# Attention and conv FFN on one core: z as [hi;hi] and [lo;lo], diagonal triangle transposed, planes landing as words

## The chip, the cores and the metric

One core of one Trainium2 chip runs the whole problem. The metric is device time in microseconds. The kernel before takes 1581.85 us, the median of three runs from 1581.26 to 1582.96.

## The reference, cut to what matters

For each of 4 batches, with S = 3136 positions, 256 value columns and 64 columns in z:

```python
scores = (1/S) * z @ z.T
attn   = maximum(scores, 0) ** 2
x      = u * (attn @ v)
h      = maximum(x @ w_in, 0)                  # 256 -> 1024
c      = conv of h along S, three taps per column (conv_w)
out    = (h * sigmoid(c)) @ w_out              # 1024 -> 256
```

The scores are symmetric: the score of key i for query j is that of key j for query i.

## The kernel before

A batch is cut into 6 blocks of 512 queries and a remainder of 64. The 24 blocks follow each other. Each meets 25 tiles of 128 keys (the last holds 64 keys twice), one tile a slot: 600 slots in all. Every fp32 operand of a matmul is split into a high part that TensorE takes in one pass and a low part (x - high); products are hi*hi, hi*lo and lo*hi, the scores all four.

z lies feature by partition. `za` holds [hi;lo] over its 128 partitions and `zb` holds [lo;hi], so that two matmuls, `za` and `zb` as weights against `za` as moving operand, sum all four products (`scores`, L290 and L291). `prep_z` (L158) fills them by half tiles of 64 partitions.

A tile is computed or transposed. A computed one has `scores`, `relu` (L342, ScalarE, PSUM bank s to SBUF tile t), `square` (L353, VectorE, or ScalarE in some early slots), `split_hi` (L360, ScalarE, tile ah), `split_lo` (L366, by the helper at L143, VectorE, tile al) and `attend` (L382, six matmuls into the two av banks). A tile whose mirror image an earlier block has already computed is taken from there. When that earlier block had its relu tile, `part` (L310, GpSimd) cut its fp32 words into two planes of 16-bit halves, pl, and `spill` (L320) wrote them to a DRAM tile dq, one plane behind the other. Later `fetch` (L328) brings the tile back by a transposing DMA of 16-bit elements into tp, with the two planes side by side, and `join` (L334, GpSimd) weaves the halves into words, tj. From these ScalarE makes the square in a PSUM bank (L339) and ah (L358); no scores matmul is needed. The tiles on the diagonal, four of each block, are computed in full.

`entries` (L110) gives the order of tiles in a block: the half tile first, the transposed ones spread evenly among the computed ones. In block q of a batch 4q tiles are transposed (fewer in the first batch, whose blocks 1 to 3 compute the first four key tiles again).

Each slot of the loop at L865 issues, in this order: `split_hi` and `split_lo` of slot k+2, `relu` and `square` of k+3, the planned work of the slot, `fetch` of k+9, `join` of k+5, `part` of k+2, `spill` of k+1, then `attend` of k and `scores` of k+4. Each engine works through its own share in that order, and so does the queue of SyncE, which issues nearly all DMAs. The framework adds the waits. A tile with a tag takes one of that tag's `bufs` buffers, and its first writer waits until one is free: s has 2, ah and al 4, t, pl, tp and tj 3 each.

The FFN of block b runs inside block b+1: `gate_x` (L490) and `split_x` (L512) turn av into xh and xl, the two xl halves on GpSimd; then eight groups of columns pass `ffn_in` (L531 to L534), relu, three taps, sigmoid, gate, split and `ffn_out` (L604 to L606). The 64 remaining queries of a batch are gathered by `rem_fetch`, `rem_join`, `rem_scores` and others around the last block. `tail` plans the end.

Of the kernel before, what the change touches and what calls it, by code (L numbers as in the profile page):

```python
# [8 lines left out]
F32 = mybir.dt.float32  # L9
# [19 lines left out]
LA, LT, LS = 4, 3, 2  # L29
LD, LJ, LP, LX = 9, 5, 2, 1  # L30

# [28 lines left out]
T_XL = "VV"  # L60

R_F, R_J, R_D, R_U, R_T = -14, -10, -12, -6, 13


@with_exitstack
def kernel(
# [43 lines left out]
    def entries(b, q):  # L110
        n, m = q * CB, min(own(b, q), q * CB)
        cs, ts = list(range(m)) + list(range(n, NJ)), list(range(m, n))
        if b or q:
            cs.insert(0, cs.pop())
        n = len(ts)
        return [
            (ts.pop(0), True) if (i + 1) * n // NJ > i * n // NJ else (cs.pop(0), False)
            for i in range(NJ)
        ]

# [5 lines left out]

    za = const.tile([P, NJ * P], F32R, name="za")
    zb = const.tile([P, NJ * P], F32R, name="zb")
    vv = const.tile([P, NJ, 2, D], F32R, name="vv")
# [27 lines left out]

    def prep_z(q, half):  # L158
        c = slice(q * NB, min((q + 1) * NB, S))
        t = zst.pop(q) if half else zst[q]  # L160
        g = nc.gpsimd
        if half == 0:
            copy(nc.scalar, za[LO, c], t[LO])
            sub(g, zb[LO, c], t[LO], za[LO, c])
            return
        copy(nc.scalar if q % 2 else nc.vector, zb[HI, c], t[HI])
        sub(g, za[HI, c], t[HI], zb[HI, c])
        if q == QB:

            for x in (za, zb):  # L170
                g.tensor_copy(x[:, S : S + HALF], x[:, S - HALF : S].bitcast(F32))

    def first_z():
        t, h = zst.pop(0), P
        v, g = nc.vector, nc.gpsimd
        c = slice(0, NB)
        copy(nc.scalar, zb[HI, c], t[HI])
        copy(v, za[LO, c], t[LO])
        sub(v, za[HI, c], t[HI], zb[HI, c])
        sub(g, zb[LO, :h], t[LO, :h], za[LO, :h])  # L180
        sub(v, zb[LO, h:NB], t[LO, h:], za[LO, h:NB])

# [111 lines left out]
    rl, pl, dq, tp, tj = {}, {}, {}, {}, {}  # L294


    def rows_of(b, r):
        if (b, r) not in dq:
            n, c = (NB, r * NB) if r < QB else (RQ, RB * NB)
            dq[b, r] = dr.tile([2, n, c], U16, tag=f"dq{r}", name=f"dq{r}")  # L300
        return dq[b, r]

    def part(k):
        blk, j, tr = at_slot(k)
        b, q = divmod(blk, QB)
        r = j // CB
        if tr or r < (Q0 if b == q == 0 else q + 1) or (r == QB and q >= RB):
            return
        pl[k] = wk.tile([P, 2, NB], U16, tag="pl", name="pl", bufs=3)
        nc.gpsimd.tensor_copy(pl[k], rl.pop(k).bitcast(U16).rearrange("p (n h) -> p h n", h=2))  # L310

    def spill(k):
        blk, j, _ = at_slot(k)
        b, q = divmod(blk, QB)
        if k not in pl:
            return
        r, p = j // CB, pl.pop(k)
        a, n = j * P - r * NB, min(P, S - j * P)
        d = rows_of(b, r)[:, a : a + n, q * NB : (q + 1) * NB]
        nc.sync.dma_start(out=d.rearrange("h p n -> p h n"), in_=p[:n])  # L320

    def fetch(k):
        blk, j, tr = at_slot(k)
        b, q = divmod(blk, QB)
        if tr:
            tp[k] = wk.tile([P, 1, 2 * NB], U16, tag="tp", name="tp", bufs=3)
            src = rows_of(b, q)[:, :, j * P : (j + 1) * P].rearrange("h r c -> (h r) c")
            nc.sync.dma_start_transpose(tp[k], src)  # L328

    def join(k):  # L330
        if k in tp:
            t = tp.pop(k)[:, 0].rearrange("p (h n) -> p h n", h=2)
            tj[k] = wk.tile([P, NB], F32, tag="tj", name="tj", bufs=3)
            nc.gpsimd.tensor_copy(tj[k].bitcast(U16).rearrange("p (n h) -> p h n", h=2), t)  # L334
# [50 lines left out]

    rt, rs, rr = {}, {}, {}
    RN = [range(i * CB, min(i + 2, RB) * CB) for i in range(0, RB, 2)] + [range(RB * CB, NJ)]

    def rem_picks():
        t = wk.tile([P, RQ], F32, tag="tj", name="pk", bufs=3)  # L390
        nc.gpsimd.memset(t, 0.0)
# [11 lines left out]
    def rem_fetch(b, i):  # L403
        n = len(RN[i])
        rt[i] = wk.tile([P, n, 2 * RQ], U16, tag="pl", name="rt", bufs=3)
        c = RN[i][0] * P
        nc.sync.dma_start_transpose(rt[i], rows_of(b, QB)[:, :, c : c + n * P].rearrange("h r c -> (h r) c"))

    def rem_join(i):
        n = len(RN[i])  # L410
        rs[i] = t = wk.tile([P, NB], F32, tag="t", name="rj", bufs=3)[:, : n * RQ]
        nc.gpsimd.tensor_copy(
            t.bitcast(U16).rearrange("p (c n h) -> p c h n", h=2, n=RQ),
            rt.pop(i).rearrange("p c (h n) -> p c h n", h=2),
        )

    def rem_scores(i):
        p = ps.tile([P, 512], F32, tag="ph", name="ph", bufs=2)
        r = za[:, QB * NB : S]
        for x, j in enumerate(RN[i]):  # L420
            w, o = slice(j * P, (j + 1) * P), p[:, x * RQ : (x + 1) * RQ]
            nc.tensor.matmul(o, lhsT=za[:, w], rhs=r, start=True, stop=False)
            nc.tensor.matmul(o, lhsT=zb[:, w], rhs=r, start=False, stop=True)
        rr["p"] = p
# [115 lines left out]
    def ffn_halo(blk, f):  # L540
        if blk == "r":
            hb[blk, f] = t = wk.tile([P, RW], F32, tag="tj", name="hr", bufs=3)
            nc.gpsimd.tensor_copy(seam(t)[:, :, 0:2], ends[:, f])
# [109 lines left out]
    for q in range(2, QB + 1):  # L653
        s = 4 * q - LA - 3 if q < QB else 4 * QB - LA - 4
        at(max(s - 4, -LA), POST, load_z, 0, q)
        at(s, POST, prep_z, q, 0)
        at(s, POST, prep_z, q, 1)
    at(-3, POST, prep_z, 1, 0)
    at(-3, POST, prep_z, 1, 1)
    for j in range(2, NJ, 2):  # L660
# [191 lines left out]
    with tc.manual_schedule():  # L852
# [12 lines left out]
        for k in range(-LA, NS):  # L865
# [79 lines left out]
```

## Time and profile before

| | |
|---|---|
| median of three runs | 1581.85 us |
| time of the profiled execution | 1582.39 us |
| its span, first to last instruction | 1580.5 us |
| its instructions | 22342 |
| chain that ended last: TensorE, ScalarE, GpSimd, VectorE | 83%, 7%, 4%, 3% |
| DMA packets, bytes | 352826, 175.70 MB |

The profiled execution lies 1.9 us over its span and 0.5 us over the median. A busy share counts the time in which an engine has an instruction in work; instructions of TensorE overlap, so that the mean duration of one is longer than the distance from one to the next.

### The profile page before, as it was taken

Reading aid. Unit: us, or ns where it says so; the run is one execution under the profiler, and the core shown is the slowest. Engines: PE = TensorE matmul, PEld = TensorE weight load, DVE = VectorE, ACT = ScalarE, POOL = GpSimd, SP = SyncE. Lnnn points to the kernel's source line nnn. Section 1 sums busy time; section 2 is a strip of 40 time slices with the busy share of each in tenths; the row PEclk is TensorE's granted clock in tenths of the full one; section 3 lists DMA queues with packets and bytes.
Section 4 is the critical chain, followed back from the end, with each engine's and each line's share of the span. In section 5 each row is a group of like instructions: output and inputs, shape, how many; then the busy total and the mean of one; then the engine's idle time right before and its main releaser. Section 6 shows DMA issues by size and latency. Waiting matters only on the chain.

```text
span 1580.5 us, 22342 instructions
## 1 busy us (share of the span) xinstructions
PE 1558.8 (99%) x6868; PEld 1275.0 (81%) x6868; DVE 1093.0 (69%) x1680; ACT 1244.3 (79%) x2329; POOL 1109.1 (70%) x1325
## 2 busy tenths in 40 slices
PE   8999999999999999999999999999999999999998
PEld 6677887878888888888888888887888888888787
DVE  7787776656777766656777776665677777666567
ACT  8898777878777877878877777787887777778767
POOL 7675567977866766778775676777875666767753
PEclk9999999999999999999999999999999999999999
DMA  5432434554434445456343444454633334546521
GB/s 162 130 120 64 117 81 112 136 124 105 140 102 122 114 87 132 106 126 138 97 141 97 110 119 105 126 113 94 155 109 111 114 93 125 105 93 133 103 54 35
DMA packets 352826, 175.70 MB, mean 111 GB/s; under 512 B 260545, under 2 KB 337345, under 8 KB 352705
## 3 DMA queue, kind: packets, MB, share of 16 engines
q1 hardware_dynamic: 352032, 173.88, 43.8%
q8 instruction: 53, 0.87, 0.2%
q14 instruction: 69, 0.56, 0.1%
q10 hardware_dynamic: 672, 0.40, 0.1%
HBM read 36.59 MB, written 75.24 MB: 71 GB/s over the span
## 4 chain that ended last, share of the span: by engine, by line
PE 83%; ACT 7%; POOL 4%; DVE 3%; issue 2%; DMA 0%; POOLq 0%; ACTq 0%; DVEq 0%
PE av L382 42%; PE ph L534 5%; PE o L606 5%; PE o L604 5%; PE s L290 5%; PE o L605 5%; PE ph L531 5%; PE ph L532 5%; PE s L291 5%; PE av L447 1%; POOL xl L143 1%; POOL tj L334 1%; DVE ph L573 1%; ACT t L342 1%; DVE al L143 1%
## 5 line engine op out<-in xcount | busy, mean ns | idle before, releaser
L382 PE MATMUL av<-ah,vv 128*128 128x512 f32 x2400 | 739.6, 391 | 4.6 <-DVE ut L499 1.9
L143 DVE TENSOR_TENSOR al<-s,ah 128x512 fp32r<-128x512 f32 x576 | 397.7, 690 | 272.3 <-ACT ah L358 203.9
L382 PEld LDWEIGHTS av<-ah,vv 128*128 128x128 f32 x2400 | 449.3, 188 | 102.5 <-DVE ut L499 2.7
L382 PE MATMUL av<-al,vv 128*128 128x512 f32 x1152 | 449.7, 390 | 0.8 <-DVE al L143 0.6
L353 DVE TENSOR_TENSOR s<-s,t 128x512 f32<-128x512 f32 x350 | 244.2, 698 | 175.4 <-ACT t L342 174.0
L334 POOL COPY tj<-tp 128x1024 uint16<-128x1024 uint16 x228 | 307.8, 1359 | 0.0
L342 ACT ACTIVATE t<-s 128x512 f32<-128x512 f32 x372 | 222.6, 598 | 101.3 <-PE s L291 88.5
L360 ACT CAST ah<-s 128x512 fp32r<-128x512 f32 x372 | 218.9, 588 | 102.1 <-DVE s L353 101.4
L573 DVE SCALAR_TENSOR_TENSOR ph<-hb,cw,ph 128x512 f32<-128x512 f32 x384 | 287.0, 747 | 7.4 <-ACT ph L568 6.7
L143 POOL TENSOR_TENSOR gl<-hb,gh 128x512 fp32r<-128x512 f32 x192 | 248.7, 1295 | 52.6 <-ACT gh L146 51.1
L310 POOL COPY pl<-t 128x1024 uint16<-128x1024 uint16 x248 | 256.5, 1039 | 7.6 <-DMA dq<-pl 7.1
L382 PEld LDWEIGHTS av<-al,vv 128*128 128x128 f32 x1152 | 216.5, 188 | 48.8 <-DVE al L143 3.9
L563 POOL COPY halo<-hb 128x2 f32<-128x2 f32 x160 | 30.1, 188 | 208.1 <-ACT hb L558 207.2
L290 PE MATMUL s<-za 128*128 128x512 f32 x372 | 148.7, 400 | 9.7 <-DVE za L143 5.1
L531 PE MATMUL ph<-xh,wih 128*128 128x512 f32 x384 | 149.8, 390 | 0.6 <-DVE hb L587 0.6
L532 PE MATMUL ph<-xh,wil 128*128 128x512 f32 x384 | 149.6, 390 | 0.0
L604 PE MATMUL o<-gh,wol 128*128 128x512 f32 x384 | 149.6, 390 | 0.0
L605 PE MATMUL o<-gh,woh 128*128 128x512 f32 x384 | 149.5, 389 | 0.0
L606 PE MATMUL o<-gl,woh 128*128 128x512 f32 x384 | 149.5, 389 | 0.0
L339 ACT ACTIVATE s<-tj 128x512 f32<-128x512 f32 x228 | 136.5, 599 | 15.7 <-POOL tj L334 15.7
L291 PE MATMUL s<-za,zb 128*128 128x512 f32 x372 | 145.9, 392 | 0.0
L358 ACT ACTIVATE ah<-tj 128x512 fp32r<-128x512 f32 x228 | 143.4, 629 | 0.3
(113 smaller groups left out, 2031.1 us busy)
## 6 DMA issues: line engine op xcount, KB each, us to landing
dq<-pl SPq DMA_DIRECT2D x228, 256.0 KB, 2.5
vst<-in_v_dram SPq DMA_DIRECT2D x48, 256.0 KB, 3.1
ut<-in_u_dram SPq DMA_DIRECT2D x24, 512.0 KB, 4.3
out_dram<-ob SPq DMA_DIRECT2D x19, 512.0 KB, 3.6
st<-in_z_dram SPq DMA_DIRECT2D x24, 256.0 KB, 3.1
tp<-dq SPq DMA_TRANSPOSE x228, 3.4
dq<-pl SPq DMA_DIRECT2D x20, 128.0 KB, 2.6
wr<-in_moe_w_in_dram SPq DMA_DIRECT2D x8, 256.0 KB, 3.1
```

The source lines that it names most:

```text
L143: eng.tensor_tensor(out=out, in0=a, in1=b.bitcast(F32), op=ALU.subtract)
L310: nc.gpsimd.tensor_copy(pl[k], rl.pop(k).bitcast(U16).rearrange("p (n h) -> p h n", h=2))
L334: nc.gpsimd.tensor_copy(tj[k].bitcast(U16).rearrange("p (n h) -> p h n", h=2), t)
L342: nc.scalar.activation(rl[k], sc[k][:, :NB], AF.Relu, scale=SC1)
L353: nc.vector.tensor_tensor(out=s, in0=s, in1=rl[k], op=ALU.mult)
L382: nc.tensor.matmul(o, lhsT=w[:, j, d], rhs=r, start=first and i == 0, stop=last and i == len(ops) - 1)
L531: nc.tensor.matmul(o, lhsT=wih[:, dc, w], rhs=xh[blk][:, dc], start=(dc == 0), stop=False)
L532: nc.tensor.matmul(o, lhsT=wil[:, dc, w], rhs=xh[blk][:, dc], start=False, stop=False)
L573: nc.vector.scalar_tensor_tensor(out=c, in0=hb[blk, f][:, k : e + k], scalar=cw[:, f, k : k + 1], in1=c, op0=ALU.mult, op1=ALU.add,)
L604: nc.tensor.matmul(o, lhsT=wol[:, f, d], rhs=h, start=(f == 0), stop=False)
L605: nc.tensor.matmul(o, lhsT=woh[:, f, d], rhs=h, start=False, stop=False)
L606: nc.tensor.matmul(o, lhsT=woh[:, f, d], rhs=l, start=False, stop=(f == FC - 1))
```

## The change

z is kept as `zh` = [hi;hi] and `zl` = [lo;lo]: `prep_z` needs one copy on ScalarE and one subtraction on GpSimd over 128 partitions in place of two of each kind over 64. The moving operand [hi;lo] of a block becomes a tile of its own, `zq`, which two DMAs from `zh` and `zl` fill eight slots before the block. In every block but the first, the four diagonal tiles stand at slots 1, 8, 15 and 22 of the block. Diagonal tile x computes only the columns from 128x on; the columns left of the diagonal are those of the earlier diagonal tiles, spilled to a DRAM tile `below` and fetched by a transposing DMA (`fetch_side`, five slots ahead). The DRAM tiles keep the two halves of a row next to each other, so that the transposed halves land as words; `join` and `rem_join` go. `fetch` runs eight slots ahead, tp has five buffers. The x tile of the gate joins the ring t, and one xl half goes from GpSimd to VectorE.

```diff
-LD, LJ, LP, LX = 9, 5, 2, 1
+LD, LE, LP, LX, LB = 8, 5, 2, 1, 5
+DG = [1, 8, 15, 22]
+ZQ = 4
...
     def entries(b, q):
         n, m = q * CB, min(own(b, q), q * CB)
-        cs, ts = list(range(m)) + list(range(n, NJ)), list(range(m, n))
-        if b or q:
-            cs.insert(0, cs.pop())
...
+        if not b and not q:
+            return [(j, False) for j in range(NJ)]
+        fixed = {0: NJ - 1, **{p: n + x for x, p in enumerate(DG)}}
+        cs, ts = list(range(m)) + list(range(n + CB, NJ - 1)), list(range(m, n))
...
+    def side(k):
+        blk, j, tr = at_slot(k)
+        x = j - blk % QB * CB
+        return x if blk and not tr and 0 <= x < CB else None
...
-    def prep_z(q, half):
+    def prep_z(q):
         c = slice(q * NB, min((q + 1) * NB, S))
...
+        t, g = zst.pop(q), nc.gpsimd
+        copy(nc.scalar, zh[:, c], t)
+        sub(g, zl[:, c], t, zh[:, c])
...
+    def query(blk):
+        b, q = divmod(blk, QB)
+        zq[blk] = t = mv.tile([P, NB], F32R, tag="zq", name="zq", bufs=2)
+        c = slice(q * NB, (q + 1) * NB)
+        nc.sync.dma_start(out=t[LO].bitcast(F32), in_=zh[LO, c].bitcast(F32))
+        nc.sync.dma_start(out=t[HI].bitcast(F32), in_=zl[HI, c].bitcast(F32))
...
-        w = slice(j * P, (j + 1) * P)
-        r = za[:, blk % QB * NB : (blk % QB + 1) * NB]
-        nc.tensor.matmul(s, lhsT=za[:, w], rhs=r, start=True, stop=False)
-        nc.tensor.matmul(s, lhsT=zb[:, w], rhs=r, start=False, stop=True)
+        w, c = slice(j * P, (j + 1) * P), (side(k) or 0) * P
+        r = zq[blk][:, c:]
+        nc.tensor.matmul(s[:, c:], lhsT=zh[:, w], rhs=r, start=True, stop=False)
+        nc.tensor.matmul(s[:, c:], lhsT=zl[:, w], rhs=r, start=False, stop=True)
...
-            dq[b, r] = dr.tile([2, n, c], U16, tag=f"dq{r}", name=f"dq{r}")
+            dq[b, r] = dr.tile([n, 2, c], U16, tag=f"dq{r}", name=f"dq{r}")
...
+    def below(blk):
+        if blk not in dd:
+            dd[blk] = dr.tile([NB - P, 2, NB - P], U16, tag="dd", name="dd")
+        return dd[blk]
...
+        r, x = j // CB, side(k)
+        if x is not None and x < CB - 1:
+            src = rl[k][:, (x + 1) * P :]
...
-        pl[k] = wk.tile([P, 2, NB], U16, tag="pl", name="pl", bufs=3)
-        nc.gpsimd.tensor_copy(pl[k], rl.pop(k).bitcast(U16).rearrange("p (n h) -> p h n", h=2))
+        n = src.shape[-1]
+        pl[k] = wk.tile([P, 2, NB], U16, tag="pl", name="pl", bufs=3)[:, :, :n]
+        nc.gpsimd.tensor_copy(pl[k], src.bitcast(U16).rearrange("p (n h) -> p h n", h=2))
...
-        d = rows_of(b, r)[:, a : a + n, q * NB : (q + 1) * NB]
-        nc.sync.dma_start(out=d.rearrange("h p n -> p h n"), in_=p[:n])
+        if x is None:
+            d = rows_of(b, r)[a : a + n, :, q * NB : (q + 1) * NB]
+        else:
+            d = below(blk)[a : a + n, :, x * P :]
+        nc.sync.dma_start(out=d, in_=p[:n])
...
+            t = wk.tile([P, 1, 2 * NB], U16, tag="tp", name="tp", bufs=LB)
+            src = rows_of(b, q)[:, :, j * P : (j + 1) * P].rearrange("r h c -> (r h) c")
+            nc.sync.dma_start_transpose(t, src)
+            tp[k] = t[:, 0].bitcast(F32)
+
+    def fetch_side(k):
+        x = side(k)
+        if x:
+            t = wk.tile([P, 1, 2 * NB], U16, tag="tp", name="tp", bufs=LB)
+            src = below(k // NJ)[: x * P, :, (x - 1) * P : x * P].rearrange("r h c -> (r h) c")
+            nc.sync.dma_start_transpose(t[:, :, : 2 * x * P], src)
+            tp[k] = t[:, 0].bitcast(F32)
...
     def relu(k):
-        if at_slot(k)[2]:
-            sc[k] = ps.tile([P, 512], F32, tag="s", name="s", bufs=2)
-            nc.scalar.activation(sc[k][:, :NB], tj[k], AF.Square, scale=SC1**-0.5)
+        x = side(k)
+        if at_slot(k)[2] or x:
+            if x:
+                rl[k] = tp[k]
+                nc.scalar.activation(tp[k][:, x * P :], sc[k][:, x * P : NB], AF.Relu, scale=SC1)
+            else:
+                sc[k] = ps.tile([P, 512], F32, tag="s", name="s", bufs=2)
+            nc.scalar.activation(sc[k][:, :NB], tp[k], AF.Square, scale=SC1**-0.5)
             return
...
-        if k in rl and not act_squares(k):
+        if k in rl and k not in tp and not act_squares(k):
...
-        if k in tj:
-            nc.scalar.activation(ah[k], tj.pop(k), AF.Square, scale=SC1**-0.5)
+        if k in tp:
+            nc.scalar.activation(ah[k], tp.pop(k), AF.Square, scale=SC1**-0.5)
...
-        x = wk.tile([P, NB], F32, tag="x1", name="x1", bufs=1)
+        x = wk.tile([P, NB], F32, tag="t", name="x1", bufs=3)
...
+    for blk in range(1, NBLK):
+        at(blk * NJ - LA - ZQ, POST, query, blk)
...
-        at(k0 + XS, C_XS, split_x, blk, (G, G))
+        at(k0 + XS, C_XS, split_x, blk, (V, G))
...
             if 0 <= k + LD < NS:
                 fetch(k + LD)
-            if 0 <= k + LJ < NS:
-                join(k + LJ)
+            if 0 <= k + LE < NS:
+                fetch_side(k + LE)
```

The remainder follows suit: its planes land as words in a pl buffer and are squared there in place, and its query tile comes by two DMAs as well.

## Rows read from the trace of the kernel before

**Rows 1.** The page, part 1: busy us, share of the span, instructions.
```profile
PE 1558.8 (99%) x6868; PEld 1275.0 (81%) x6868; DVE 1093.0 (69%) x1680; ACT 1244.3 (79%) x2329; POOL 1109.1 (70%) x1325
```

**Rows 2.** Windows: stretch, its us, busy us (x instructions) by engine, granted clock, DMA share, GB/s.
```profile
63.20:66.20 3.00, 3.00 (x8) 2.30 (x7) 1.34 (x4) 2.22 (x5) 0.73 (x1) 0.50 0.27 86
...
400.00:500.00 100.00, 100.00 (x442) 82.51 (x441) 74.06 (x112) 76.16 (x139) 68.48 (x83) 1.00 0.42 123
640.70:701.50 60.80, 60.66 (x271) 49.75 (x270) 39.07 (x59) 51.62 (x98) 49.70 (x56) 1.00 0.49 113
```

**Rows 3.** Waits of TensorE, whole span: waiter, releaser, us in total, times, longest.
```profile
PE s L290 <- DVE za L143: 5.1, 1, 5.1
PE s L290 <- DVE al L143: 4.2, 8, 1.1
...
PE ph L534 <- POOL xl L143: 1.1, 4, 0.3
```

**Rows 4.** Timeline of TensorE at the first block boundary: idle before it, and its releaser.
```profile
62.26 0.74 PE L382 MATMUL av<-ah,vv 128*128 128x512 f32 x2 [1.57 <-DVE ut L499]
```

**Rows 5.** Timeline of TensorE, 64-column matmuls: the 2nd and the 10th of ten.
```profile
291.49 0.28 PE L423 MATMUL ph<-za,zb 128*128 128x64 f32 x1
...
292.38 0.28 PE L423 MATMUL ph<-za,zb 128*128 128x64 f32 x1
```

**Rows 6.** Timeline of TensorE, 256-column matmuls: the first and the seventh of twelve.
```profile
1540.44 0.28 PE L531 MATMUL ph<-xr,wih 128*128 128x256 f32 x1
...
1541.15 0.28 PE L531 MATMUL ph<-xr,wih 128*128 128x256 f32 x1
```

**Rows 7.** Groups by line and shape, ScalarE: count | busy us, mean ns | idle before, releasers.
```profile
L342 ACT ACTIVATE t<-s 128x512 f32<-128x512 f32 x372 | 222.6, 598 | 101.3 <-PE s L291 88.5 <-POOL gl L143 5.8 <-POOL pl L310 2.7
L360 ACT CAST ah<-s 128x512 fp32r<-128x512 f32 x372 | 218.9, 588 | 102.1 <-DVE s L353 101.4
L358 ACT ACTIVATE ah<-tj 128x512 fp32r<-128x512 f32 x228 | 143.4, 629 | 0.3
L339 ACT ACTIVATE s<-tj 128x512 f32<-128x512 f32 x228 | 136.5, 599 | 15.7 <-POOL tj L334 15.7
...
L556 ACT ACTIVATE hr<-ph 128x256 f32<-128x256 f32 x8 | 2.9, 380 | 0.1
```

**Rows 8.** Groups by line and shape, VectorE.
```profile
L143 DVE TENSOR_TENSOR al<-s,ah 128x512 fp32r<-128x512 f32 x576 | 397.7, 690 | 272.3 <-ACT ah L358 203.9 <-ACT ah L360 63.0 <-PE av L382 2.0
...
L353 DVE TENSOR_TENSOR s<-s,t 128x512 f32<-128x512 f32 x350 | 244.2, 698 | 175.4 <-ACT t L342 174.0
```

**Rows 9.** Groups by line and shape, GpSimd.
```profile
L334 POOL COPY tj<-tp 128x1024 uint16<-128x1024 uint16 x228 | 307.8, 1359 | 0.0
L310 POOL COPY pl<-t 128x1024 uint16<-128x1024 uint16 x248 | 256.5, 1039 | 7.6 <-DMA dq<-pl 7.1
...
L143 POOL TENSOR_TENSOR xl<-ut,xh 128x512 fp32r<-128x512 f32 x46 | 59.3, 1313 | 73.2 <-ACT xh L146 73.2
```

**Rows 10.** Timeline of ScalarE, block 11: the write of one slot's ah.
```profile
722.10 0.62 ACT L358 ACTIVATE ah<-tj 128x512 fp32r<-128x512 f32 x1
```

**Rows 11.** Timeline of TensorE: the attend matmuls that read that ah.
```profile
727.78 0.62 PE L382 MATMUL av<-ah,vv 128*128 128x512 f32 x2
```

**Rows 12.** Timeline of SyncE's queue, block 11: start, us of issue.
```profile
727.94 1.16 SPq L328 DMA_TRANSPOSE tp<-dq  x1
729.16 0.59 SPq L188 DMA_DIRECT2D vst<-in_v_dram  x1
```

**Rows 13.** DMA issues by line: count, KB each, median us from issue to landing.
```profile
dq<-pl SPq DMA_DIRECT2D x228, 256.0 KB, 2.5
...
tp<-dq SPq DMA_TRANSPOSE x228, 3.4
```

**Rows 14.** Waits of SyncE's queue, whole span.
```profile
SPq L320 <- POOL pl L310: 453.1, 172, 13.8
SPq L328 <- POOL tj L334: 200.8, 71, 11.9
```

More of the change, by code (lines that the diff above doesn't have):

```diff
@@ L111, in entries @@
         n, m = q * CB, min(own(b, q), q * CB)
-        cs, ts = list(range(m)) + list(range(n, NJ)), list(range(m, n))
-        if b or q:
-            cs.insert(0, cs.pop())
[L115 to L119, printed above, removed]
+        if not b and not q:
+            return [(j, False) for j in range(NJ)]
+        fixed = {0: NJ - 1, **{p: n + x for x, p in enumerate(DG)}}
+        cs, ts = list(range(m)) + list(range(n + CB, NJ - 1)), list(range(m, n))
+        i, t, order = 0, len(ts), []
+        for p in range(NJ):
+            if p in fixed:
+                order.append((fixed[p], False))
+                continue
+            f = NJ - len(fixed)
+            order.append((ts.pop(0), True) if (i + 1) * t // f > i * t // f else (cs.pop(0), False))
+            i += 1
+        return order
     ent = [[entries(b, q) for q in range(QB)] for b in range(B)]
@@ L156, in load_z, with query_rem @@
         zst[q] = t[:, :w]
-    def prep_z(q, half):
+    def prep_z(q):
         c = slice(q * NB, min((q + 1) * NB, S))
[L160 to L167, printed above, removed]
+        t, g = zst.pop(q), nc.gpsimd
+        copy(nc.scalar, zh[:, c], t)
+        sub(g, zl[:, c], t, zh[:, c])
         if q == QB:
-            for x in (za, zb):
+            for x in (zh, zl):
                 g.tensor_copy(x[:, S : S + HALF], x[:, S - HALF : S].bitcast(F32))
+    zq = {}
+    def query(blk):
[4 more added lines that the diff above has]
+        nc.sync.dma_start(out=t[HI].bitcast(F32), in_=zl[HI, c].bitcast(F32))
+    def query_rem(b):
+        zq["r"] = t = mv.tile([P, RQ], F32R, tag="zr", name="zr", bufs=1)
+        nc.sync.dma_start(out=t[LO].bitcast(F32), in_=zh[LO, QB * NB : S].bitcast(F32))
+        nc.sync.dma_start(out=t[HI].bitcast(F32), in_=zl[HI, QB * NB : S].bitcast(F32))
     def first_z():
         t, h = zst.pop(0), P
[L175 to L181, printed above, removed]
+        v, g, a = nc.vector, nc.gpsimd, nc.scalar
+        zq[0] = x = mv.tile([P, NB], F32R, tag="zq", name="zq", bufs=2)
+        copy(a, zh[:, :h], t[:, :h])
+        copy(v, x, t)
+        sub(g, zl[:, :h], t[:, :h], zh[:, :h])
+        copy(a, zh[:, h:NB], t[:, h:])
+        sub(v, x[HI], t[HI], x[HI])
+        sub(v, zl[:, h:NB], t[:, h:], zh[:, h:NB])
     def load_v(b, j):
@@ L305, in part @@
         b, q = divmod(blk, QB)
-        r = j // CB
-        if tr or r < (Q0 if b == q == 0 else q + 1) or (r == QB and q >= RB):
+        r, x = j // CB, side(k)
+        if x is not None and x < CB - 1:
+            src = rl[k][:, (x + 1) * P :]
+        elif x is None and not (tr or r < (Q0 if b == q == 0 else q + 1) or (r == QB and q >= RB)):
+            src = rl[k]
+        else:
             return
-        pl[k] = wk.tile([P, 2, NB], U16, tag="pl", name="pl", bufs=3)
-        nc.gpsimd.tensor_copy(pl[k], rl.pop(k).bitcast(U16).rearrange("p (n h) -> p h n", h=2))
+        n = src.shape[-1]
+        pl[k] = wk.tile([P, 2, NB], U16, tag="pl", name="pl", bufs=3)[:, :, :n]
+        nc.gpsimd.tensor_copy(pl[k], src.bitcast(U16).rearrange("p (n h) -> p h n", h=2))
     def spill(k):
@@ L316, in spill @@
             return
[L317 removed]
+        r, p, x = j // CB, pl.pop(k), side(k)
         a, n = j * P - r * NB, min(P, S - j * P)
[L319 to L320 removed]
+        if x is None:
[3 more added lines that the diff above has]
+        nc.sync.dma_start(out=d, in_=p[:n])
     def fetch(k):
@@ L384, in attend @@
                 )
-    rt, rs, rr = {}, {}, {}
+    rs, rr = {}, {}
     RN = [range(i * CB, min(i + 2, RB) * CB) for i in range(0, RB, 2)] + [range(RB * CB, NJ)]
     def rem_picks():
-        t = wk.tile([P, RQ], F32, tag="tj", name="pk", bufs=3)
+        t = wk.tile([P, RW], F32, tag="t", name="pk", bufs=3)[:, :RQ]
         nc.gpsimd.memset(t, 0.0)
@@ L404, in rem_fetch @@
         n = len(RN[i])
-        rt[i] = wk.tile([P, n, 2 * RQ], U16, tag="pl", name="rt", bufs=3)
+        t = wk.tile([P, n, 2 * RQ], U16, tag="pl", name="rt", bufs=3)
         c = RN[i][0] * P
[L407 to L415, printed above, removed]
+        nc.sync.dma_start_transpose(t, rows_of(b, QB)[:, :, c : c + n * P].rearrange("r h c -> (r h) c"))
+        rs[i] = t.rearrange("p c n -> p (c n)").bitcast(F32)
     def rem_scores(i):
         p = ps.tile([P, 512], F32, tag="ph", name="ph", bufs=2)
-        r = za[:, QB * NB : S]
+        r = zq["r"]
         for x, j in enumerate(RN[i]):
             w, o = slice(j * P, (j + 1) * P), p[:, x * RQ : (x + 1) * RQ]
-            nc.tensor.matmul(o, lhsT=za[:, w], rhs=r, start=True, stop=False)
-            nc.tensor.matmul(o, lhsT=zb[:, w], rhs=r, start=False, stop=True)
+            nc.tensor.matmul(o, lhsT=zh[:, w], rhs=r, start=True, stop=False)
+            nc.tensor.matmul(o, lhsT=zl[:, w], rhs=r, start=False, stop=True)
         rr["p"] = p
@@ L541, in ffn_halo @@
         if blk == "r":
-            hb[blk, f] = t = wk.tile([P, RW], F32, tag="tj", name="hr", bufs=3)
+            hb[blk, f] = t = wk.tile([P, RW], F32, tag="t", name="hr", bufs=3)
             nc.gpsimd.tensor_copy(seam(t)[:, :, 0:2], ends[:, f])
```

26 lines of the change are left out of this document (8 added, 18 removed).

## The prediction

> **What bounds the kernel now.** I read the page's busy line first [rows 1]: TensorE is busy 99% of the span, ScalarE 79%, GpSimd 70%. Since a busy TensorE need not be a fast one, I went to the windows [rows 2]: in the stretch from 400 to 500 us it is never idle and issues 442 matmuls, 100 us / 442 = 226 ns each, at a granted clock of 1.00, the 2.4 GHz level. That is the cadence of a 512-column matmul here, and nearly all of the 6868 are of that width. The waits of TensorE [rows 3] say how much is not cadence: 5.1 us once, at the start, 4.2 us in eight waits of the scores for a score bank that VectorE frees late, 1.1 us for xl; the other waits of that view are each shorter than 2 us, and most of the total lies ahead of 135 us. So a microsecond taken out of the matmul stream is a microsecond off the time, and a microsecond off GpSimd is worth nothing unless TensorE was waiting for it.
>
> One stall costs more than its length. At the first block boundary TensorE stood for 1.57 us [rows 4]; from 63.2 to 66.2 us the granted clock was 0.50, the 1.2 GHz level, and 8 matmuls ran where 13 do [rows 2]. That is some 1.5 us more.
>
> **Part by part.**
>
> *Narrower scores.* In each of the 23 blocks after the first, three diagonal tiles lose 128, 256 and 384 columns, in two matmuls each. Prices by width, start to start: 64 columns, (292.38 - 291.49) / 8 = 111 ns [rows 5]; 256 columns, (1541.15 - 1540.44) / 6 = 118 ns [rows 6]; 512 columns, 226 ns. A matmul of 128 columns lies between 111 and 118, I take 115. One of 384 has no row; it lies between 118 and 226, and I take the middle, 172, since from 256 to 512 the price nearly doubles with the width. Per block: 2 x [(226 - 172) + (226 - 118) + (226 - 115)] = 2 x 273 = 546 ns; times 23, **12.6 us**. With 384 columns at 226 or at 118 it is 10.1 or 15.0.
>
> *The other engines' share of a diagonal tile.* ScalarE gets an extra Square of 599 ns for each of three tiles (square left VectorE), its ah costs 629 in place of 588, and its relu shrinks by the columns left out; with 380 ns for 256 columns and 598 for 512 [rows 7] that is 0.85 ns a column, 768 columns, 0.65 us. Per block 1.80 + 0.12 - 0.65 = +1.27 us, 29 us in all. VectorE loses three squares of 698 ns and gains one xl of 690 [rows 8]: -1.4 us a block. GpSimd loses all 228 joins, 307.8 us, half of the xl, 30 us, and half of the z subtractions; it gains three parts of 384, 256 and 128 columns, by the 1039 ns of a full one 1.56 us a block, 36 us [rows 9]. All this is beside TensorE and enters the sum at nothing. Its cover: in block 10, one of the tightest, ScalarE is busy 51.6 of 60.8 us [rows 2], so 1.27 us fits into 9.2 us idle; and ah is ready early. The ah written from 722.10 to 722.72 [rows 10] is read at 727.78 [rows 11], the writes and the attends counted from the start: 5.1 us ahead, two slots. Without that cover ScalarE's share alone would cost 29 us.
>
> *xl half on VectorE.* The first FFN of a block waited for xl 1.1 us in all [rows 3]; two halves in a row on GpSimd took 2 x 1.31 us [rows 9], now they run side by side. Bounds 0 and -1.1; I take -1.0. Behind the VectorE half queue the squares and al of the next slot, 0.69 us later; ah and al are far ahead, so nothing.
>
> *The x tile of the gate goes into the ring of relu tiles.* The second relu after the gate must wait until GpSimd has done the gate's multiply and a part behind it. The wait stands on ScalarE, and the split and FFN work queues behind it. About 0.5 us at each boundary from the durations, inside the 5.1 us lead: nothing.
>
> *Queues.* Per block SyncE gets three more spills and two query copies at about 0.59 us and three more transposes at 1.16 us [rows 12]: 6.4 us of some 61. Landing takes 2.5 and 3.4 us [rows 13]. The query is issued eight slots before the block, four before the first scores read it: four slots of 60.8 / 25 = 2.43 us, 9.7 us, against 1.2 + 2.5 us. Nothing, unless the queue is held up: the first scores wait then, and TensorE with them.
>
> *The new wait.* ScalarE's Square of a diagonal tile waits for a transpose issued at program slot p-5 and used at p-3, two slots or 4.9 us later; and the transpose waits for the spill of the tile before (issued three slots earlier, 2.5 us to land) and for one of the five landing buffers, which ScalarE now frees at its second Square, no longer GpSimd at the join. In the last block of a batch, with six transposed tiles in a row, the buffer for slot 8 comes free with the split of slot 6, in program slot 4, and ScalarE wants the data in slot 5. One slot, 2.4 us, against 3.4 us to land and up to 1.16 us behind another transpose: ScalarE stands for 1.0 to 2.2 us, twice in each of four such blocks. Behind it queue ah of the next slot and the FFN's relu, tap and sigmoid; TensorE waits for none of them before the 5.1 us are used up, but its scores need a bank freed by al about one slot ahead, and there 1.1 us stalls are on record [rows 3]. Bounds 0 and 8 x 1.2 = 10 us; I take +1.0, near the low end, because the lead is longer than the wait.
>
> **The sum.** 1582.39 - 12.6 - 1.0 + 1.0 = 1569.8 us. The profiled execution was 0.5 us over the median of 1581.85, so **1569.3 us**. What a measurement of this kernel can tell from no change is about 0.2%, 3.2 us: faster means below 1578.7.
>
> **Rivals.**
>
> *The side transposes hold TensorE up (slower).* Place: ScalarE's Square of a diagonal tile, 69 of them. For it: SyncE already stands 453 us behind GpSimd's parts and 201 us behind its joins, up to 13.8 us at a time [rows 14], and a fetch held for a buffer holds the spills and queries behind it, in a queue where two slots, not four, lie between issue and use. Against it: joins, which SyncE waited for, are gone. It decides from 12.6 / 69 = 0.18 us of TensorE idle per tile. At half a slot less lead, some 0.4 us a tile lost, 28 us: 1597 us; more if the clock falls as at the first boundary [rows 2]. Chance 0.09.
>
> *The gain is paid back (no change).* Held fetches delay the spills, three pl buffers then hold GpSimd's parts, and the three relu tiles hold ScalarE. At one 0.5 us stall of TensorE in each of 23 blocks, 11.5 us: 1581 us. For it: the 453 us; against it: the part reads an early tile, and TensorE lost only some 16 us to waits in all. Chance 0.07.
>
> *Narrow matmuls cost only their columns (faster still).* If the weight load hides behind the neighbour, 128 columns follow the line from 512 to 256, 0.42 ns a column: 64 ns in place of 115, 2.3 us more, 1567 us. Against it: ten in a row stay at 111 ns [rows 5]. The Trainium skill (TensorE: Matmul & The Clock Gate, Back-to-back issue gap) gives the gap as N/2.4 + 2.5 ns, 56 ns at 128 columns, and says itself that this leaves out the weight load; by it the saving would be 2 x 320 x 23 ns, an estimate of 14.7 us. Chance 0.05.
>
> **How the numbers follow.** My forecast has 0.79. Its own range: 1569.3 less 2.4 for cheap 384-column matmuls and some 3 us if a lighter ScalarE and VectorE close part of the early stalls, 1563; plus 2.5 for dear ones and 5 for half the bound of the new wait, 1577. That holds the third rival too: 0.84, so the range is 1563 to 1577. Faster: 0.79 + 0.05, less 0.01 for the edge, 0.83; same 0.08; slower 0.09.
>
> **What would show it.** Right: score matmuls of 384, 256 and 128 columns, 46 each, followed after about 172, 118 and 115 ns; no tj; GpSimd under 810 us, ScalarE up by 20 to 30; TensorE's waits still under 20 us. Wrong: TensorE waiting for al or ah at the diagonal slots, ScalarE idle for the transposes by far over 1 us each, or a block that has not become 0.5 us shorter. A granted clock of 0.50 inside the span would mean stalls that I did not see.

## The result, and the profile after

The changed kernel takes 1565.47 us, the median of four runs (1564.47 to 1567.35), beside 1582.22 us for the kernel before on the same chip (four runs). The ratio is 0.9896, 95% interval 0.9881 to 0.9911: 16.8 us or 1.0% faster. The forecast was 1569.3 with 1563 to 1577. The profiled execution took 1564.48 us, its span is 1562.7, 17.8 less than before.

The page of the changed kernel, part 1, answers to [rows 1]:

```profile
PE 1544.1 (99%) x6868; PEld 1270.7 (81%) x6868; DVE 1052.2 (67%) x1621; ACT 1255.5 (80%) x2385; POOL 791.1 (51%) x1104
```

GpSimd went from 1109 to 791 us, under the 810 of the prediction, and VectorE from 1093 to 1052. ScalarE rose by 11 us and not by the 20 to 30 that were named as a sign: the durations of its instructions add up to 19.6 us more, some 28 for the diagonal tiles less 7 for the z copies, which the prediction's term for ScalarE left out, and busy time counts what overlaps only once. TensorE is busy 99% again, with 14.7 us less. The groups of its score matmuls, by shape:

```profile
L312 PE MATMUL s<-zq,zh 128*128 128x512 f32 x303 | 120.8, 399 | 8.9 <-DVE zq L155 5.1 <-DVE al L155 3.7
...
L312 PE MATMUL s<-zq,zh 128*128 128x384 f32 x23 | 7.7, 333 | 0.0
...
L312 PE MATMUL s<-zq,zh 128*128 128x256 f32 x23 | 6.4, 278 | 0.0
...
L312 PE MATMUL s<-zq,zh 128*128 128x128 f32 x23 | 5.4, 234 | 0.2 <-DVE al L155 0.2
```

Each narrow width stands there 23 times on this line and as often on L313. Their means are durations; the distance from one to the next is read from the timeline of TensorE, here a tile of 128 columns in block 12:

```profile
808.42 0.22 PE L312 MATMUL s<-zq,zh 128*128 128x128 f32 x1
808.48 0.28 PE L313 MATMUL s<-zq,zl 128*128 128x128 f32 x1
808.60 0.45 PE L567 MATMUL ph<-xh,wih 128*128 128x512 f32 x1
808.88 0.39 PE L568 MATMUL ph<-xh,wil 128*128 128x512 f32 x1
809.11 0.39 PE L567 MATMUL ph<-xh,wih 128*128 128x512 f32 x1
```

The pair's own distances are 0.06 and 0.12 us, and the 512-column matmul that follows holds its successor to 0.28 in place of 0.23. Together the pair costs 0.46 - 0.23 = 0.23 us, 115 ns each, the price taken from [rows 5, 6]. A distance read at one matmul alone would have been wrong.

TensorE's waits, the whole list, answer to [rows 3]:

```profile
PE s L312 <- DVE zq L155: 5.1, 1, 5.1
PE s L312 <- DVE al L155: 3.9, 6, 1.8
PE av L425 <- DVE ut L535: 1.7, 2, 1.4
PE av L425 <- ACT x L530: 1.3, 1, 1.3
PE av L425 <- DVE ah L155: 0.7, 1, 0.7
PE ph L567 <- DVE hb L623: 0.6, 1, 0.6
PE ph L567 <- DVE xr L513: 0.3, 1, 0.3
```

The list adds up to 13.6 us, against 16.0 before: by it, the waits hardly moved. The distances say otherwise. For each block I took the time from its first attend matmul to the next block's (block 0 from the first matmul of all, block 23 to the last), and took off its matmuls at the distances of an undisturbed stream (512 columns 226.7 ns, 384 173, 266 124, 256 117, 128 115, 64 112). What is left is what TensorE lost, in us. The table, worked out from the traces, serves all that follows (blocks 4, 10, 16, 22 are the fifth, 5, 11, 17 the sixth of a batch):

```
kernel                        block 0  block 1  4,10,16,22  5,11,17  others   sum
before                           8.15     7.42        4.63     5.10    6.72  32.0
changed                          5.65     8.27        2.19     6.11    4.54  26.8
  full width                     4.69     7.12        1.86     4.89    3.89  22.5
  no triangle                    5.00     9.54        1.86     2.33    3.86  22.6
  old z                          8.41    10.54        2.36     3.97    5.36  30.6
  xl on GpSimd                   5.39     9.65        5.12     8.08    7.94  36.2
  side lead 7                    4.71     8.49        2.11     2.48    4.60  22.4
  side lead 7, full width        4.72     8.43        1.90     2.29    3.86  21.2
  side lead 7, old z             9.40     8.49        2.01     2.46    5.34  27.7
  side lead 7, weights later     4.72    11.41        2.06     2.40    4.59  25.2
  side lead 4                    5.48    10.78        2.26    15.45    5.21  39.2
before, xl on VectorE            8.11     6.15        1.91     2.80    5.69  24.7
before, words, no rem_join       8.12     7.42       15.90     3.17    6.28  40.9
before, words                    9.70     6.68        2.91     3.20    6.08  28.6
```

Blocks 0 and 1 hold a stall and a fall of the clock. Block 0 differs by up to 1.6 us between kernels that are the same there, and block 1 by 2 us or more between kernels whose edit lies elsewhere; a single profile does not tell how much of that would repeat. The other columns repeat to some 0.2 us.

One wait is new, ScalarE's. Its line in the list of waits, and the late diagonal tile at slot 15 of block 11 in the timelines of ScalarE and of SyncE's queue:

```profile
ACT s L382 <- DMA tp<-dd: 16.5, 9, 4.0
```

```profile
726.32 0.38 ACT L379 ACTIVATE tp<-s 128x256 f32<-128x256 f32 x1
729.80 0.60 ACT L382 ACTIVATE s<-tp 128x512 f32<-128x512 f32 x1 [3.09 <-DMA tp<-dd]
```

```profile
724.09 1.16 SPq L363 DMA_TRANSPOSE tp<-dq  x1
725.35 1.20 SPq L371 DMA_TRANSPOSE tp<-dd  x1
```

ScalarE finished its relu at 726.70 and stood for 3.09 us; the transpose that it wanted had been issued at 725.35, right behind another one. The ah of this tile was still written by 731.95 and read at 734.22, 2.3 us later; even after the longest of these waits, 4.0 us in block 17, 1.3 us were left. What TensorE lost in such a block it lost elsewhere, at scores that wait for a bank, here in block 11 behind its second late tile:

```profile
749.92 0.50 PE L312 MATMUL s<-zq,zh 128*128 128x512 f32 x1 [0.23 <-DVE al L155]
```

### The profile page after: what moved, and what is told of

It reads as the page before. It is cut to its first block, busy times and chain, and to the rows that moved or that the text cites. A ratio compares the mean times of both kernels' runs of the same rounds, so it can differ in the third digit from the quotient of the medians.

```text
span 1562.7 us, 22596 instructions
## 1 busy us (share of the span) xinstructions
PE 1544.1 (99%) x6868; PEld 1270.7 (81%) x6868; DVE 1052.2 (67%) x1621; ACT 1255.5 (80%) x2385; POOL 791.1 (51%) x1104
## 4 chain that ended last, share of the span: by engine, by line
PE 90%; ACT 4%; DMA 2%; DVE 1%; issue 1%; POOL 1%; ACTq 0%; SPq 0%; DVEq 0%; POOLq 0%
PE av L425 47%; PE ph L567 5%; PE ph L570 5%; PE ph L568 5%; PE o L642 5%; PE o L640 5%; PE o L641 5%; PE s L312 5%; PE s L313 5%; PE av L483 2%; DMA tp<-dd 1%; ACT s L382 1%; ACT ah L401 1%; ACT hb L594 1%; ACT ph L604 1%
## 5 line engine op out<-in xcount | busy, mean ns | idle before, releaser
L396 DVE TENSOR_TENSOR s<-s,t 128x512 f32<-128x512 f32 x283 | 197.5, 698 | 161.5 <-ACT t L385 160.5
L342 POOL COPY pl<-t 128x1024 uint16<-128x1024 uint16 (+1 forms) x271 | 276.2, 1021 | 2.2 <-POOL hb L586 1.6
L385 ACT ACTIVATE t<-s 128x512 f32<-128x512 f32 x303 | 181.6, 599 | 100.8 <-PE s L313 90.8
L403 ACT CAST ah<-s 128x512 fp32r<-128x512 f32 x303 | 178.4, 589 | 68.7 <-DVE s L396 68.5
L382 ACT ACTIVATE s<-tp 128x512 f32<-128x512 f32 x297 | 176.9, 596 | 18.4 <-DMA tp<-dd 16.5
L401 ACT ACTIVATE ah<-tp 128x512 fp32r<-128x512 f32 x297 | 186.1, 627 | 0.3
L312 PE MATMUL s<-zq,zh 128*128 128x512 f32 (+1 forms) x372 | 140.2, 377 | 9.1 <-DVE zq L155 5.1
L594 ACT ACTIVATE hb<-ph 128x512 f32<-128x512 f32 x192 | 114.4, 596 | 32.9 <-PE ph L570 31.5
L313 PE MATMUL s<-zq,zl 128*128 128x512 f32 (+1 forms) x372 | 139.9, 376 | 0.0
```

The lines of the kernel that those rows point to most:

```text
L312: nc.tensor.matmul(s[:, c:], lhsT=zh[:, w], rhs=r, start=True, stop=False)
L313: nc.tensor.matmul(s[:, c:], lhsT=zl[:, w], rhs=r, start=False, stop=True)
L342: nc.gpsimd.tensor_copy(pl[k], src.bitcast(U16).rearrange("p (n h) -> p h n", h=2))
L401: nc.scalar.activation(ah[k], tp.pop(k), AF.Square, scale=SC1**-0.5)
```

## The experiments

Theory 1 was the prediction's: the time follows the matmul columns, and the other engines are beside them. Theory 2: the gain came from lighter engines. All runs have the kernel before beside them.

**Full width.** The diagonal scores run over 512 columns again, with all the rest of the change.

```diff
-        w, c = slice(j * P, (j + 1) * P), (side(k) or 0) * P
+        w, c = slice(j * P, (j + 1) * P), 0
```

> The changed kernel (1565.5 us median), but the scores matmuls of the diagonal tiles again run over all 512 columns; spill, fetch and everything on the other engines stay. Theory 1, the time follows the matmul columns: per block 2 x [(226 - 172) + (226 - 118) + (226 - 115)] = 546 ns come back, 12.6 us in 23 blocks, so 1578.1 us (1577 to 1579.5). Theory 2, the gain came from lighter GpSimd, VectorE and ScalarE: hardly slower, 1565 to 1569 us.

Measured 1573.97 us (ratio to before 0.9953, 0.9939 to 0.9967). Neither theory: 8.5 us of the gain went, and 8.1 us stayed although TensorE had every column back. In the blocks that nothing disturbs (7 and 20, for instance) the block became 0.50 us longer, near the 0.546 of the prediction; 23 x 0.50 = 11.5. The rest of the difference is for the most part in blocks 0, 1 and 5, 11, 17.

**No triangle.**

```diff
-        return x if blk and not tr and 0 <= x < CB else None
+        return None
```

> The changed kernel without the triangle: diagonal tiles at the same slots, computed in full, squared on VectorE, neither spilled nor fetched. Theory 1: the matmul columns come back, 12.6 us, and the transposes that ScalarE waited for are gone, which held TensorE by some 1 us at most, so 1577 to 1578 us, the same as with full width alone or up to 1 us less. The rival, that the spill, fetch and wait of the triangle cost TensorE far more than that: 5 us or more below the run with full width alone. Theory 2 (lighter engines): 1565 to 1569 us.

Measured 1571.52 us (0.9933, 0.9921 to 0.9945), in none of the three ranges: 2.5 us below full width, and the intervals of the two meet. In the table blocks 5, 11 and 17 lose 2.33 in place of 4.89 us, but block 1 loses 9.54 in place of 7.12, so that the sums are the same. Spill, fetch and wait of the triangle cost TensorE 2.6 us in the last blocks of a batch and next to nothing in the others behind block 1; that they cost the 2.5 us of the medians is not shown.

**Old z.** `za` and `zb` come back as the kernel before has them: `prep_z` and `first_z` by halves, no `query`, no `query_rem`.

```diff
-        r = zq[blk][:, c:]
-        nc.tensor.matmul(s[:, c:], lhsT=zh[:, w], rhs=r, start=True, stop=False)
-        nc.tensor.matmul(s[:, c:], lhsT=zl[:, w], rhs=r, start=False, stop=True)
+        r = za[:, blk % QB * NB + c : (blk % QB + 1) * NB]
+        nc.tensor.matmul(s[:, c:], lhsT=za[:, w], rhs=r, start=True, stop=False)
+        nc.tensor.matmul(s[:, c:], lhsT=zb[:, w], rhs=r, start=False, stop=True)
...
-            at(s, POST, prep_z, q)
+            at(s, POST, prep_z, q, 0)
+            at(s + 2, POST, prep_z, q, 1)
...
-        at(blk * NJ - LA - ZQ, POST, query, blk)
```

> The changed kernel with z kept as before, in two tiles [hi;lo] and [lo;hi] filled by halves, and no query copies; triangle, words and xl stay. Block 0 of the changed kernel is 2.5 us shorter than before though its matmuls are the same. Theory 1: that is the z work which ScalarE, VectorE and GpSimd no longer do while TensorE waits for them, so the 2.5 us come back: 1568.0 us (1567 to 1569.5). Rival: the block got shorter by something else, and the z layout is worth nothing: 1565.5 us (1564.5 to 1566.5). A second rival, that half-tile z work held TensorE in every batch: 1570 us or more.

Measured 1567.49 us (0.9909, 0.9896 to 0.9923), 2.0 us more, within Theory 1's range, but the interval meets that of the changed kernel. Block 0 lost 8.41 us in place of 5.65 and block 1 10.54 in place of 8.27; blocks 5 and 17 lost 2 us less than with the new z. With the late transposes out of the way, below, the price is clearer.

**Both xl halves on GpSimd.**

```diff
-        at(k0 + XS, C_XS, split_x, blk, (V, G))
+        at(k0 + XS, C_XS, split_x, blk, (G, G))
```

> The changed kernel with both xl halves on GpSimd. Theory 1: TensorE waits for xl at some block boundaries again, 1.0 us in all, a little more with the gaps that follow such a wait: 1566.5 us (1566 to 1568). Rival: with joins gone GpSimd is early enough, nothing: 1565.5 us. Second rival: the half on VectorE delays al, above all in block 1, where TensorE stands 1.8 us for it, and putting it back gains 1 us: 1564.5 us.

Measured 1573.86 us (0.9948, 0.9935 to 0.9960): 8.4 us more, where 1.0 was expected. The list of TensorE's waits and one of them in its timeline:

```profile
PE ph L570 <- POOL xl L155: 5.0, 8, 0.7
```

```profile
709.46 0.40 PE L570 MATMUL ph<-xl,wih 128*128 128x512 f32 x1
710.53 0.50 PE L570 MATMUL ph<-xl,wih 128*128 128x512 f32 x1 [0.67 <-POOL xl L155]
```

The second matmul starts 1.07 us after the first, 0.84 more than in the stream, but its idle is given as 0.67: a wait counts from the modelled end of the matmul before, 0.40 us after its start, and the stream's distance is 0.23. So every wait costs some 0.17 us more than the list says, the matmul after it adds 0.1, and a short wait does not stand in the list at all: at 581.8 us two xl matmuls start 0.49 us apart, and neither list nor timeline shows a wait. By the distances TensorE lost 9.5 us at the first xl matmuls of the 23 blocks in this run, 7.3 of them at the eight waits of the list, against 1.6 in the changed kernel: 7.9 of the 8.4.

**Words alone, on the kernel before.** The DRAM tiles become `[n, 2, c]`, `join` and `rem_join` go, the fetch lead is 8, tp has five buffers.

```diff
-            tp[k] = wk.tile([P, 1, 2 * NB], U16, tag="tp", name="tp", bufs=3)
-            src = rows_of(b, q)[:, :, j * P : (j + 1) * P].rearrange("h r c -> (h r) c")
-            nc.sync.dma_start_transpose(tp[k], src)
+            t = wk.tile([P, 1, 2 * NB], U16, tag="tp", name="tp", bufs=LB)
+            src = rows_of(b, q)[:, :, j * P : (j + 1) * P].rearrange("r h c -> (r h) c")
+            nc.sync.dma_start_transpose(t, src)
+            tj[k] = t[:, 0].bitcast(F32)
...
-            at(k5 + R_J + 2 * i, POST, rem_join, i)
```

> The kernel before (1582.1 us) with one part of the change: the planes land as words, joins and the remainder's joins are gone (308 + 14 us of GpSimd), fetches run 8 slots ahead into five buffers. z, order of tiles, full diagonal tiles and both xl halves on GpSimd stay. Theory 1: GpSimd is not what TensorE waits for, apart from xl, and xl stays late without joins too (the run with xl back on GpSimd), so 1580 to 1582.5 us. Theory 2 (a lighter GpSimd carries the gain): 1574 us or less.

Measured 1591.81 us (1.0060, 1.0048 to 1.0073): 9.8 us slower than before. Waits of GpSimd, ScalarE and TensorE:

```profile
POOL pl L310 <- DMA dq<-pl: 23.0, 5, 5.9
```

```profile
ACT ph L556 <- POOL hb L538: 12.5, 4, 3.4
```

```profile
PE s L290 <- DVE al L143: 10.9, 7, 2.5
```

Without `rem_join` the remainder's three fetches keep their pl buffers until its squares are split. The part of a tile then stands up to 5.9 us on GpSimd, the FFN's halo copy queues behind it, ScalarE's tap waits for the copy, al is late, TensorE's scores find no bank: the chain of the prediction's second rival, in four blocks, but started by the remainder and not by SyncE. The changed kernel has the wait on GpSimd too, in the same four blocks, at the part of a diagonal tile:

```profile
POOL pl L342 <- DMA dq<-pl: 11.1, 4, 4.0
```

There it goes no further: no tap waits for the halo copy in ScalarE's list, and the four blocks lose 2.19 us in all.

**Words alone, with the remainder as before.** As above, but `rem_join` stays as a plain copy of the words.

```diff
-        rs[i] = t.rearrange("p c n -> p (c n)").bitcast(F32)
+        rt[i] = t.rearrange("p c n -> p (c n)").bitcast(F32)
+
+    def rem_join(i):
+        n = len(RN[i])
+        rs[i] = t = wk.tile([P, NB], F32, tag="t", name="rj", bufs=3)[:, : n * RQ]
+        nc.gpsimd.tensor_copy(t, rt.pop(i))
...
+            at(k5 + R_J + 2 * i, POST, rem_join, i)
```

> The words alone on the kernel before, as in the run that came out at 1591.8 us, but the remainder again copies its fetched words on GpSimd into the relu ring, so that its three buffers of the ring pl come free as early as before. In that run GpSimd stood up to 5.9 us for a pl buffer, and blocks 4, 10, 16 and 22, where the remainder holds them, were 2 to 4 us longer. Theory 1: that is all of its loss, and the words are worth what blocks 5, 11 and 17 showed, 0.6 us each: 1580 to 1582 us. Rival: words cost or give by themselves (fetches one slot later, ScalarE at the landing buffers): 1585 us or more, or 1575 us or less.

Measured 1578.16 us (0.9973, 0.9962 to 0.9983): the loss is gone, and 4.5 us of gain appear, more than Theory 1 and less than its rival allowed. The 4.5 us include whatever the fetch lead of 8 and the five buffers give. The waits of TensorE for al fell from 4.2 us in eight to 2.5 in three.

**One xl half on VectorE, alone on the kernel before.**

```diff
-        at(k0 + XS, C_XS, split_x, blk, (G, G))
+        at(k0 + XS, C_XS, split_x, blk, (V, G))
```

> The kernel before with one edit: one xl half on VectorE. The list of waits shows only 1.1 us for xl before, and I priced it by that. Putting xl back in the changed kernel cost 8.4 us, though, and TensorE's distance from matmul to matmul, summed over blocks 2 to 22, is 8 us more before than in the changed kernel without the triangle. Theory 1: a wait costs TensorE more than the gap that the list shows, and xl is most of those 8 us: 1575 to 1578 us. Rival: xl costs before what the list shows, and the 8.4 us belong to the changed kernel alone (its new order or its rings): 1580.5 to 1582 us.

Measured 1576.49 us (0.9965, 0.9952 to 0.9977), 5.5 us faster by one letter of the code and within Theory 1. The kernel before at a block boundary, and the waits of ScalarE and TensorE in this run:

```profile
715.42 0.39 PE L534 MATMUL ph<-xl,wih 128*128 128x512 f32 x1
716.07 0.50 PE L534 MATMUL ph<-xl,wih 128*128 128x512 f32 x1 [0.27 <-POOL xl L143]
```

```profile
ACT s L339 <- POOL tj L334: 5.1, 7, 0.8
```

```profile
PE s L290 <- DVE al L143: 2.5, 4, 1.1
```

By the distances TensorE lost 3.7 us at the first xl matmuls of the blocks before, where the list has 1.1, and 0.3 in this run. No wait for xl is left in the list, and two others shrank with it: ScalarE's for a join from 15.7 us [rows 7] to 5.1, and TensorE's for al from 4.2 us [rows 3] to 2.5. The joins of a block's first slots stood on GpSimd behind 2.6 us of xl. The two prices, 5.5 for xl and 4.5 for the words, are in part of the same waits and don't add.

**Diagonal transposes seven slots ahead, and four.**

```diff
-LD, LE, LP, LX, LB = 8, 5, 2, 1, 5
+LD, LE, LP, LX, LB = 8, 7, 2, 1, 5
```

> The changed kernel with the diagonal transposes issued seven slots ahead in place of five. Theory 1: in the last block of a batch they come too late for ScalarE (waits of 1.0 to 4.0 us, 16.5 us in all) and cost TensorE 2.5 to 3.8 us in blocks 5, 11 and 17 together; two slots earlier they land in time: 1562 to 1563.5 us. Rival: issued one slot after the spill that they read, they hold SyncE's queue for its landing, and nothing is gained or 1 to 2 us lost: 1565 to 1567.5 us.

Measured 1559.51 us (0.9856, 0.9841 to 0.9871): 6.0 us faster than the changed kernel, more than Theory 1 gave it, and the best of all. ScalarE has no wait for tp left in its list, and blocks 5, 11 and 17 lose 2.48 us in place of 6.11; the rest of the 6.0 is in block 0 and in what the medians of runs scatter. With `LE` at 4:

> The changed kernel with the diagonal transposes issued four slots ahead: one slot, some 2.4 us, less. Theory 1: the lead of ah over its use, 5 us, covers most of it, and TensorE loses 0.5 to 2 us more in each of blocks 5, 11 and 17 and little elsewhere: 1567 to 1571 us. The slower rival of the prediction, in which each late diagonal tile holds TensorE by 0.4 us: 69 tiles, 28 us, 1593 us.

Measured 1576.84 us (0.9966, 0.9953 to 0.9978), between the two ranges. ScalarE's list:

```profile
ACT s L382 <- DMA tp<-dd: 44.3, 23, 4.8
```

Of 69 diagonal tiles with a fetched part only 23 made ScalarE wait. TensorE paid in blocks 5, 11 and 17 (15.5 us lost, against 6.1), perhaps in block 1 (10.8 against 8.3), and hardly in the others. The slower rival's mechanism is there, a slot from where the change put it, but its cost is bound to blocks with six fetched tiles in a row. Block 23 has such rows and such waits as well and lost only 0.4 us more; why is open.

**Lead 7, with full width and with the old z.** The two edits from above on the better kernel.

> The changed kernel with the diagonal transposes seven slots ahead (1559.5 us) and the diagonal scores over all 512 columns: the price of the columns without the late transposes. By the term of the prediction 12.6 us more, 1572.1 us; by the undisturbed blocks of the run with full width at five slots (0.50 us a block, 23 blocks) 11.5 us, 1571.0 us. Theory 2, lighter engines: under 1565 us.

Measured 1571.58 us (0.9930, 0.9917 to 0.9942): 12.1 us for the columns, between the two numbers expected.

> The changed kernel with the diagonal transposes seven slots ahead (1559.5 us) and z kept as before in two half-filled tiles, without query copies. With five slots the old z came out only 2.0 us slower, but its block 0 was 2.8 us longer and its blocks 5 and 17 were 2 us shorter, where the diagonal transposes are late. Theory 1: block 0 alone, now without that offset: 1562 to 1563.5 us. Rival: the query copies cost as much elsewhere as block 0 gains: 1559 to 1560.5 us.

Measured 1565.31 us (0.9893, 0.9877 to 0.9910): 5.8 us for the z layout, more than the 2.5 to 4 of Theory 1. Block 0 has 4.7 of it; windows of the old z and of the new one, from 5 to 50 us:

```profile
5.00:50.00 45.00, 43.74 (x171) 33.86 (x172) 38.41 (x72) 39.23 (x82) 38.46 (x39) 1.00 0.52 157
```

```profile
5.00:50.00 45.00, 44.82 (x189) 36.49 (x190) 37.85 (x74) 40.05 (x86) 36.53 (x38) 1.00 0.60 177
```

The new z lets 18 more matmuls into the same 45 us at the same granted clock. That the old z was dear in block 0 in every kernel that has it (8.1 to 9.7 in the table, against 4.7 to 5.7) makes the place shown; which of the three engines' z work held TensorE wasn't separated.

**Weight preparation two slots later, at lead 7.**

```diff
-WS = [0, 4, 8, 12, 16, 20, 24, 26, 28, 30, 32, 36, 40, 44, 48, 52]
+WS = [0, 4, 8, 12, 16, 20, 26, 28, 30, 32, 34, 36, 40, 44, 48, 52]
```

> The changed kernel with the diagonal transposes seven slots ahead (1559.5 us), and five of the weight preparations moved two slots later, so that VectorE reaches the gate of block 0 before them: at the first boundary TensorE waits 1.3 and 1.4 us for av, and its clock falls. If that wait is VectorE's weight work, 2 to 3 us less: 1556.5 to 1558 us. Rival: the work only moves into block 1, where VectorE is as full, and is paid there: 1559 to 1561 us.

Measured 1562.17 us (0.9872, 0.9858 to 0.9885), 2.7 us more than without it, though the intervals of the two meet. Windows of this kernel, and of lead 7 as it was:

```profile
57.00:62.00 5.00, 5.00 (x24) 4.07 (x23) 3.15 (x8) 4.05 (x8) 1.65 (x2) 1.00 0.52 135
...
75.00:95.00 20.00, 17.14 (x54) 12.94 (x55) 16.64 (x28) 15.41 (x32) 13.30 (x19) 0.74 0.41 128
```

```profile
57.00:62.00 5.00, 3.56 (x11) 2.63 (x10) 3.52 (x6) 2.89 (x7) 1.64 (x2) 0.74 0.33 89
...
75.00:95.00 20.00, 17.04 (x74) 13.16 (x73) 17.83 (x29) 18.72 (x39) 14.73 (x21) 1.00 0.44 142
```

The boundary is cured: 24 matmuls in place of 11, clock at 1.00. But behind it TensorE waits for al four times:

```profile
PE s L312 <- DVE al L155: 4.9, 4, 1.9
```

That was 3.5 us in three waits without the edit. From 75 to 95 us it is idle no longer than without the edit, 2.9 us, but the granted clock averages 0.74, part of it at the 1.2 GHz level, and 54 matmuls run where 74 did. Block 1 loses 11.41 us in place of 8.49. The rival was right in kind, and the time lies 1.2 us above its range.

## Why the prediction was right, and where its steps were not

The time lies in the range and near its low end; the sum came out 3.8 us high. The largest term holds, three others were mis-sized and cancelled in part. By the runs the columns gave 12.1 us and z, xl and words together 10.4, less 6.0 for the late transposes, 16.5 of the 16.8; the sum has 12.6 and 1.0, less 1.0. That it came so near is in part luck.

*Narrower scores: right.* 12.6 us forecast, 12.1 measured where no late transpose blurs it, 0.50 us a block in undisturbed blocks, where 0.546 was forecast. The third rival, in which 128 columns cost 64 ns, fell, though the time lies nearer to its 1567 than to 1569.3 us: with what it does to its successor the matmul costs 115. The Trainium skill's formula for the gap (TensorE: Matmul & The Clock Gate, Back-to-back issue gap), which by the page has no budget for the weight load, gives 56 ns at 128 columns and, as an estimate, 14.7 us for the columns; this trace does not agree, with 115 ns and 12.1 us.

*"Bounds 0 and -1.1; I take -1.0", for xl: the step that failed most.* The run on the kernel before gave 5.5, five times the larger bound. Two reasons are shown. The bound was the list's idle time, 1.1 us, where TensorE lost 3.7 by the distances. And the step asked what VectorE's half would hold up, not what the xl on GpSimd already held up: the joins behind it, ScalarE's squares behind those, and a score bank. What each of these gave is not separated.

*"All this is beside TensorE and enters the sum at nothing."* Wrong for the words, 4.5 us alone (in part the same waits), and for the z layout, 5.8 us at lead 7. The 5.1 us lead of ah [rows 10, 11] was read at one slot well inside a block, and the gains lie elsewhere: by the table the z layout's in block 0, where the same lead has a median of 1.2 us before, the words' in the last two blocks of a batch, where the columns 4,10,16,22 and 5,11,17 fall from 4.63 to 2.91 and from 5.10 to 3.20. (The 60.8 us read as block 10 [rows 2] are not that block, whose attends run from 642.5 to 709.3 us; there ScalarE is idle for 14 us, not 9, so that its 1.27 us fit all the more.) "Some 3 us" for a lighter early part stood in the range, not in the sum.

*The new wait: right in place, mis-sized.* "ScalarE stands for 1.0 to 2.2 us, twice in each of four such blocks": it was 16.5 us in nine waits, up to 4.0. TensorE lost 3.6 us by the blocks, 6.0 by the medians, against the +1.0 taken; inside the bounds of 0 and 10. "The lead is longer than the wait" held: by the distances the attends of blocks 5, 11 and 17 lose as much with lead 7. What failed is the weight of the other path that the step names, the score bank freed by al: 2.9 of the 3.6 us stand at the scores of these blocks, and most of the rest at an FFN matmul that waits for the remainder's xr.

*The rivals.* The slower one did not happen, though the run at lead 4 shows its wait one slot away. The chain of the second, from a held pl buffer to TensorE, exists, in the run with the words alone and no `rem_join`. The part of theory 2 that is true is about half: with all the columns back, the changed kernel was still 8.1 us faster than before.

Left open: why xl on GpSimd costs more in the changed kernel (8.4) than before (5.5), although no joins are behind it. At the start of block 11, with both halves on GpSimd, both kernels have xl written 3.3 us after ScalarE begins xh; TensorE comes to it 0.4 us earlier in the changed one, and loses 0.97 us in place of 0.55. What brings it there earlier was not followed. Open too is how the 10.4 us that lead 7 gains over before beyond the columns split among z, xl and words, since the parts share waits; the new order of tiles and the x tile in the ring t were not run by themselves, and may have a share.

## What to carry to other kernels

Price a wait of TensorE by the distance from matmul to matmul, block by block, against an undisturbed block; the idle time in a list of waits is a lower bound. Before work is called hidden on an engine that isn't the bound, read what stands behind it in that engine's queue where the pipeline is shortest, at block boundaries and at the start. When work comes late, follow every buffer that it holds, not only its own result: here ah was in time and the score bank was not. When a new transfer gets a lead, count the slot in which its buffer comes free and the transfers ahead of it, and try one or two slots more: here that was worth as much as a third of the whole change.

## What the runs showed of the hardware that was not expected

A narrow matmul passes part of its cost on: after a pair of 128 columns, 58 and 112 ns apart, the 512-column matmul that follows holds its successor to 286 ns in place of 227; of the 23 pairs, 20 show these numbers, and the other three stand in blocks 5, 11 and 17, where TensorE waits. And the halves of a fetched tile, interleaved by the layout in DRAM alone, land as words at about the price of planes: 3.6 us median from issue to landing in the changed kernel, 3.4 before [rows 13].
